# Two transformer layers on one core: the second MLP product in Strassen's plain form with a bank for each product, and a readiness rule for TensorE's order

## The chip, the core and the metric

The kernel runs on one core of a Trainium2 chip. A core has five engines that work side by side, each through its own instruction stream in program order: TensorE (PE, matrix products into PSUM), VectorE (DVE), ScalarE (ACT), GpSimd (POOL) and SyncE (SP, which here only issues transfers). They wait for each other by semaphores. Sixteen DMA engines move data between the HBM and the on-chip memory SBUF; here the transfers are issued from SP's and from ACT's stream. PSUM has eight banks of 2 KB for each of the 128 partitions. The metric is the time of one launch on the device in microseconds (us), lower is better.

## What is computed

The input is one sequence of 2048 rows of 640 float32 values. Two different blocks are applied alternately, each twice and with the same weights:

```python
x = x + _A_ref(_layernorm(x), A_wqkv, A_wo)
x = x + _B_ref(_layernorm(x), B_w1, B_b1, B_w2, B_b2)
x = x + _A_ref(_layernorm(x), A_wqkv, A_wo)
x = x + _B_ref(_layernorm(x), B_w1, B_b1, B_w2, B_b2)
```

Block A is attention with 32 heads of 20 values in which a row sees itself and the 255 rows before it. Block B is an MLP: `h = x @ w1 + b1` (640 to 1536), `h = max(h, 0) ** 2`, `h @ w2 + b2` (1536 to 640).

## The kernel before

**Number format.** Most products are made of three half-precision products: each operand is split into a high and a low float16 part, and high x high, high x low and low x high are summed in PSUM. The helper `mm3` (matmuls on L323) issues such a triple for each chunk of 128.

**Units.** The rows are cut into units of 256; with two layers there are 16 units (`NU`). The stages of a unit `u` are:

- `ln_load`, `ln_cross`: load the rows, layer norm, split into two float16 parts (`yl`) and turn them by transposing DMAs on SP into `yT` (L412, L434, L438, L441). There is one `yT` buffer.
- `stage_qk`, `stage_v`: the q, k and v projections from `yT`. q and k go to the HBM and come back in the layout for attention; `stage_v` works in four quarters of 15 matmuls.
- attention, in eight quads of four heads: `max_quad` (scores on L610, row maxima by DVE on L622), `exp_quad` (scores again on L673, exponential by ACT on L686, masks by POOL on L701 and L705) and `pv_quad` (product with v on L735, copy on L747). The maxima go to the rows of q through small transfers (`qt<-mT`, L648).
- `load_o`, `stage_o`: normalise the attention output, multiply with `wo`, add to the rows (L845), second layer norm; `y_cross` turns it into `y2`.
- `stage_f`: both MLP products, described next.

**The MLP in a unit.** The first product runs in six blocks `p`, each with feature chunks p and p + 6. ACT adds the bias and clips (L914), POOL squares (L918). The second product is a 2 x 2 block product in Strassen's way, with seven products for eight. Both sides need sums of blocks: those of `w2` are made once at the start and kept in the HBM (`w2d`); those of the activations are made in every block by POOL (L926, L930, L934), and ACT and DVE split the seven results into float16 parts (L937, L941) in the tile `hh`. Then come the seven products on L977, cut into 21 pieces of six matmuls; each piece needs 320 KB of `w2d`, fetched from ACT's stream (L311) into a ring of `SLOTS` = 7 places. The fetch for piece n + 7 is queued when piece n has been used. It is Winograd's form of the scheme: the products share sums. One bank, "x", stays open through four of the products, whose partial results build up in it; "y" is opened for the other three. DVE adds each result to the rows (L993). The bias `b2` is loaded anew in each unit and added by POOL in four halves (L865).

**Banks.** Six of PSUM's eight banks serve the scores of attention. The other two are handed out by `mm_tile` to all else: projections, MLP products, `pv`, small transposes.

**What sets the order.** The order of the instructions of every engine is fixed when the program is built. The builder keeps a clock `now` for TensorE and one for each other engine, with a booked cost for each operation. `post` queues a job for an engine; `pump` places the jobs whose start has come; `need` moves `now` forward until a job is done, that is, it accepts a wait of TensorE. `together` mixes attention with a stream of "dense" work (the generators of the stages above): after every attention step it runs dense work until that has had its share of the cost (`done < cost * share * part / total`). While "y" is open it runs dense work regardless. In loop `u`, the dense stream is q, k, v of unit u + 1, then `stage_o` and `stage_f` of unit u - 1.

## Time and profile before

| | us |
|---|---|
| runs shown | 1962.94 and 1966.79, median 1964.87 |
| the profiled execution | 1978.56 |
| its span, first to last instruction | 1976.8 |
| a steady unit (1315.3 to 1432.9) | 117.6 |
| its first MLP product (1369.7 to 1405.5) | 35.8 |
| its second MLP product (1405.5 to 1435.6) | 30.1 |

The profile comes from one profiled execution. PE is TensorE's matmuls and PEld its weight loads, which overlap them. A row of a table of groups reads: line, engine, operation, output<-inputs by the program's names, shape, xcount | busy us, mean ns of one | idle time of the engine just before them and what ended it. A row of the table of waits reads: who waited <- for whom: us in total, times, longest. A row of the timeline reads: start, length, engine, line, operation, xcount, and in brackets the idle time before it with what ended it. The granted clock (PEclk) is TensorE's clock as a share of full speed.

### The profile page before, as it was taken

The page shows a single profiled execution, that of the slowest core. Times are in us where ns is not written, and L with a number is a line of the kernel's source. Part 1 is how long each engine was busy: PE and PEld are TensorE (multiplying, and loading weights), DVE is VectorE, ACT ScalarE, POOL GpSimd, SP SyncE. Part 2 cuts the span into 40 slices and gives each one's busy share as a digit, 9 for nine tenths or more (in the row PEclk, how much of TensorE's full clock was granted, in tenths as well). Part 3 has the DMA queues.
Part 4 walks back from the last instruction along what each step waited for, and adds up shares of the span by engine and source line. Part 5 has one row for each costly group of instructions (what it writes and reads, how often), then busy time and mean ns, then how long its engine had stood idle before and what let it go on. Part 6 is the DMA issues. An engine that isn't in the chain of part 4 may idle for free. (4 is left out here: it accounts for less than half of the span.)

```text
span 1976.8 us, 44962 instructions
## 1 busy us (share of the span) xinstructions
PE 1700.5 (86%) x17398; PEld 1203.1 (61%) x17398; DVE 1106.3 (56%) x3230; ACT 757.8 (38%) x1509; POOL 832.0 (42%) x1594
## 2 busy tenths in 40 slices
PE   8976878898988989888897989889898898968878
PEld 7654556565656657566574756656666565645555
DVE  8776654565646456564455656456564555735342
ACT  4644334343443434434332433434344343434312
POOL 1236425345262533625243262524526244344524
PEclk9998989899989989899898989989999899988898
DMA  9765553745538275363747437274553836424253
GB/s 257 195 193 174 146 123 75 214 95 145 151 90 202 65 200 122 99 172 75 210 98 205 111 98 179 66 209 109 136 144 93 200 80 171 108 53 138 83 176 107
DMA packets 287982, 275.12 MB, mean 139 GB/s; under 512 B 87576, under 2 KB 228504, under 8 KB 287768
## 3 DMA queue, kind: packets, MB, share of 16 engines
q1 hardware_dynamic: 227640, 145.74, 31.6%
q10 hardware_dynamic: 60128, 126.51, 21.6%
q8 instruction: 137, 2.24, 0.5%
q14 instruction: 77, 0.63, 0.1%
HBM read 194.78 MB, written 59.83 MB: 129 GB/s over the span
## 5 line engine op out<-in xcount | busy, mean ns | idle before, releaser
L622 DVE CUSTOM_DVE_ANT_0 bb<-bb,maskb 128x384 f32<-128x384 f32 (+2 forms) x1024 | 512.1, 566 | 135.1 <-PE bb L610 120.3
L686 ACT ACTIVATE pt<-bb 128x512 f32<-128x512 f32 x736 | 377.5, 599 | 352.0 <-PE bb L673 247.2
L701 POOL TENSOR_SCALAR_AFFINE_SELECT pt<-pt 128x256 f32<-128x256 f32 x448 | 190.8, 432 | 620.8 <-ACT pt L686 613.0
L323 PE MATMUL acc<-y,w_s 128*128 128x256 f16 x2880 | 358.5, 288 | 12.7 <-ACT r L914 10.8
L977 PE MATMUL acc<-ring,hh 128*128 128x320 f16 x2016 | 304.6, 308 | 45.5 <-ACT hh L937 21.1
L323 PEld LDWEIGHTS <-w_s 128*128 128x128 f16 x2880 | 293.1, 103 | 81.5 <-issue 33.9
L323 PE MATMUL acc<-yT,wq_s 128*128 128x256 f16 x2250 | 290.9, 290 | 50.7 <-DMA yT<-yl 46.8
L323 PEld LDWEIGHTS <-wq_s 128*128 128x128 f16 x2400 | 244.0, 103 | 113.6 <-DMA yT<-yl 36.0
L735 PE MATMUL pv<-pt,vt 128*32 128x128 f32 (+1 forms) x3840 | 229.3, 348 | 74.3 <-POOL pt L705 41.2
L705 POOL TENSOR_SCALAR_AFFINE_SELECT pt<-pt 128x256 f32<-128x256 f32 x512 | 240.7, 492 | 107.2 <-ACT pt L686 103.2
L977 PEld LDWEIGHTS <-hh 128*128 128x128 f16 x2016 | 194.7, 100 | 149.6 <-issue 28.9
L941 DVE TENSOR_TENSOR hh<-r,hh 128x896 f16<-128x896 f32 x96 | 114.9, 1197 | 304.1 <-ACT hh L937 304.1
L735 PEld LDWEIGHTS pv<-pt,vt 128*32 128x32 f32 x3840 | 113.7, 114 | 149.8 <-POOL pt L705 67.3
L918 POOL TENSOR_TENSOR r<-r 128x256 f32<-128x256 f32 x192 | 132.6, 710 | 101.5 <-ACT r L914 99.8
L747 ACT COPY ot<-pv 128x256 f32<-128x256 f32 x128 | 47.6, 372 | 318.1 <-PE pv L735 280.2
L937 ACT CAST hh<-r 128x896 f16<-128x896 f32 x96 | 90.1, 938 | 179.5 <-POOL r L934 170.3
L360 POOL TENSOR_TENSOR bmv<-bmv,neghalf 128x1 f32<-128x1 f32 x64 | 42.7, 668 | 260.4 <-DVE bmv L354 260.3
L323 PE MATMUL acc<-wo_s,od 128*128 128x320 f16 x960 | 142.2, 301 | 7.6 <-DVE od L821 7.3
L673 PE MATMUL bb<-qt,kt 62*128 62x128 f16 (+1 forms) x1920 | 115.9, 246 | 36.5 <-DVE mx L622 16.8
L622 DVE DVE_READ_ACCUMULATOR2_ANT mx<- 128x1 f32 x1024 | 145.3, 142 | 0.0
L610 PE MATMUL bb<-kt,qt 60*128 60x128 f16 (+1 forms) x2176 | 113.6, 245 | 27.0 <-ACT pt L686 15.1
L323 PE MATMUL acc<-wq_s,yT 128*128 128x320 f16 x900 | 133.7, 301 | 3.0 <-DVE y L373 2.3
(97 smaller groups left out, 1469.8 us busy)
## 6 DMA issues: line engine op xcount, KB each, us to landing
ring<-w2d ACTq DMA_DIRECT2D x336, 320.0 KB
qt<-qk SPq DMA_DIRECT2D x30, 480.0 KB
kt<-qk SPq DMA_DIRECT2D x30, 480.0 KB
qk<-qd SPq DMA_DIRECT2D x17, 640.0 KB
o<-ot SPq DMA_DIRECT2D x256, 42.0 KB
od<-o SPq DMA_DIRECT2D x14, 640.0 KB
qk<-yl SPq DMA_DIRECT2D x13, 640.0 KB
w2d<-ring ACTq DMA_DIRECT2D x6, 1120.0 KB
```

The lines of the kernel that those rows point to most:

```text
L323: nc.tensor.matmul(acc, lhs(a, c), rhs(b, c), start=(k == 0), stop=(k == 3 * nk - 1))
L610: nc.tensor.matmul(to, qt[r, p, i * P:(i + 1) * P], kt[r, p, a:b], start=True, stop=True)
L622: nc.vector.tensor_tensor_reduce(out=v, in0=v, in1=mask, scale=1.0, scalar=-3.0e38, op0=ALU.add, op1=ALU.max, accum_out=accum),
L673: nc.tensor.matmul(bb[e][:, k, o:o + w], kt[r, 2 * qd + j, ko:ko + P], qt[r, 2 * qd + j, q0 * P:q0 * P + w], start=True, stop=True)
L686: nc.scalar.activation(box["pt"][:, :o], bb[e][:, k, :o], AF.Exp, scale=SCALE / (QS * QS))
L701: nc.gpsimd.affine_select(out=m, in_=m, pattern=[[0, 2], [-1, P]], compare_op=ALU.is_gt, fill=0.0, base=0, channel_multiplier=1)
L705: nc.gpsimd.affine_select(out=m, in_=m, pattern=[[0, 2], [1, P]], compare_op=ALU.is_ge, fill=0.0, base=0, channel_multiplier=-1)
L735: nc.tensor.matmul(pv[32 * jj:32 * (jj + 1), q0 * P:(q0 + qn) * P], vf[:, c:c + 32], pj[:, j, :], start=(k == 0), stop=(k == len(steps) - ...
L918: nc.gpsimd.tensor_tensor(blocks(), blocks(), blocks(), op=ALU.mult)
L937: nc.scalar.copy(hs[p // 3][:, 0, p % 3], box["r"][:, 0:7])
L941: nc.vector.tensor_sub(h[:, 1, p % 3], box["r"][:, 0:7], h[:, 0, p % 3])
L977: nc.tensor.matmul(acc[:, :HD], hs[p // 3][:, a, p % 3, PLACE[j], :], ring[:, n % SLOTS, c, b, :], start=bank not in started, stop=(p == F ...
```

## The change

It has five parts.

**Plain form.** The seven products are those of Strassen's first scheme. Each has its own bank, opened at its first piece and handed back when DVE has added it. A product is added to one to two places by `outs`; where two places have the same sign, one DVE instruction writes both. Nine adds cover twelve halves, where eight covered eight. Two squares and three sums on POOL become one square on ACT, one on DVE and three sums on POOL (two of 128x256, one of 128x128).

**Order.** Generators now yield a `Want` (jobs that must be done, and whether a bank must be free) ahead of what they need. `Stream.go` runs the dense stream until its next want isn't fulfilled in the program's clock. `together` goes on with attention when the quota is reached and the step's own wants are fulfilled, or when the dense stream can't go on and they are; otherwise time passes until either can.

**Where work lies.** The next unit's rows are loaded and normalised after block p = 0 of the first product instead of after the last. In loops u = 2 to 13, v's third quarter moves behind block 5 and the fourth ahead of the third product; the transposes into `yT` wait for that (`free`).

**Memory.** `SLOTS` is 6 for 7. `b2` is loaded once and stays; it is added in two instructions of 640 columns, queued behind the second layer norm. The two row tiles x1 become one, `xb`. The tile `r` has nine blocks for eight.

**Start and end.** w1's low halves are made by POOL with one more ACT pass in place of DVE; w2's sums follow the new scheme, its loads have other staging places and a higher priority; the first half of `hh` no longer waits for w2. The dense work held back for the last two units (`CARRY`, `KEEP`) goes from 25 and 27 thousand ns to 15 and 20.

```diff
-SLOTS = 7
+SLOTS = 6
...
+    def when(w):
+
+        if any(j.end is None for j in w.jobs):
+            return None
+        t = max([0.0] + [j.end for j in w.jobs])
+        if w.bank and len(banks2) > 1:
+            free = [max(j.end for j in b) + LAT for b in banks2 if b and all(j.end is not None for j in b)]
+            if not free:
+                return None
+            t = max(t, min(free))
+        return t
...
+    class Stream:
...
+        def go(self):
+            while not self.over:
+                if self.want is not None:
+                    t = when(self.want)
+                    if t is None or t > now[0]:
+                        return None
+                    self.want = None
+                c = next(self.gen, "over")
+                if c == "over":
+                    self.over = True
+                elif isinstance(c, Want):
+                    self.want = c
+                else:
+                    step(c)
+                    return c
+            return None
...
-    PIECES = [("x", 0, 0), ("x", 0, 1), ("y", 1, 0), ("y", 1, 1), ("x", 0, 2), ("y", 1, 2)] + [
-        (b, j, g) for b, j in (("x", 2), ("y", 3), ("x", 4), ("y", 6), ("x", 5)) for g in range(3)]
-    PLACE = [0, 1, 4, 6, 5, 2, 3]
+    PRODS = [(2, 3, [(1, 3, 1, 1)]), (1, 0, [(0, 1, 1, 1), (1, 2, 1, -1)]), (0, 6, [(1, 4, 2, 1)]), (3, 2, [(1, 2, 1, 1)]),
+             (6, 4, [(0, 3, 2, 1)]), (5, 1, [(2, 3, 1, -1), (3, 4, 1, 1)]), (4, 5, [(2, 3, 1, 1)])]
+    DONE = {3: [1], 4: [0], 5: [3], 6: [2]}
+    PIECES = [(0, 0), (0, 1), (1, 0), (1, 1), (0, 2), (1, 2)] + [(k, g) for k in range(2, 7) for g in range(3)]
...
-            out.append(dma(lambda turn=turn: turn(0), P * D * 2, j, cost=1250.0, land=CROSS))
+            out.append(dma(lambda turn=turn: turn(0), P * D * 2, j, after, cost=1250.0, land=CROSS))
...
-                    def square(blocks=blocks):
-                        nc.gpsimd.tensor_tensor(blocks(), blocks(), blocks(), op=ALU.mult)
+                    def square(blocks=blocks, k=k):
+                        if k:
+                            nc.vector.tensor_tensor(blocks(), blocks(), blocks(), op=ALU.mult)
+                        else:
+                            nc.scalar.activation(blocks(), blocks(), AF.Square)
...
+            if p == 0 and ahead is not None:
+                ln_load(ahead)
+            yield from between.get(p, ())
         if ahead is not None:
-            ln_cross(ahead, *b2j)
...
+            free = Job("S", 0.0, None, [], 0.0, 0)
+            ln_cross(ahead, free)
...
+            if k == 2 and g == 0 and FP in between:
+                yield from between[FP]
+                free.end = now[0]
+            yield Want(slots[n], hj[2 * g], bank=g == 0)
+            if g == 0:
+                accs[k] = mm_tile([P, 2 * T], "acc")
...
+        def work(part, w):
+
+            nonlocal done
+            while True:
+                t = when(w) if w else None
+                ready = t is not None and t <= now[0]
+                if done >= cost * share * part / total and (ready or not w):
+                    return
+                c = s.go()
+                if c is not None:
+                    done += c
+                elif ready or (s.over and not w):
+                    return
+                else:
+                    wait_any(*([w] if w else []), *([s.want] if s.want else []))
...
-            while opened["y"]:
-                c = next(dense)
-                step(c)
-                done += c
...
-    QKC, VC, OC, FCST, LNC, CARRY, KEEP, MID = 16.4e3, 8.2e3, 8.2e3, 36.8e3, 1.2e3, 25e3, 27e3, 8e3
+    QKC, VC, OC, FCST, LNC, CARRY, KEEP, MID = 16.4e3, 8.2e3, 8.2e3, 36.8e3, 1.2e3, 15e3, 20e3, 8e3
...
-            parts += [stage_qk(u + 1, (0,)), stage_v(u + 1, range(2)), stage_o(u - 1), lambda: (y_cross(u - 1), iter(()))[1], stage_qk(u + 1, (1,)), stage_v(u + 1, range(2, 4))]
+            parts += [stage_qk(u + 1, (0,)), stage_v(u + 1, range(2)), stage_o(u - 1), lambda: (y_cross(u - 1), iter(()))[1], stage_qk(u + 1, (1,))]
+            if u < NU - 2:
+                between = {FP - 1: stage_v(u + 1, (2,)), FP: stage_v(u + 1, (3,))}
+            else:
+                parts.append(stage_v(u + 1, range(2, 4)))
             cost += QKC + VC
```

311 lines of the change are left out of this document (173 added, 138 removed).

## The prediction

> **What bounds the kernel now.** I read the page's shares first.
>
> ```profile
> span 1976.8 us, 44962 instructions
> PE 1700.5 (86%) x17398; PEld 1203.1 (61%) x17398; DVE 1106.3 (56%) x3230; ACT 757.8 (38%) x1509; POOL 832.0 (42%) x1594
> ```
>
> TensorE is the bound, with two kinds of loss: it is idle for 1976.8 - 1700.5 = 276 us, and some of its busy time runs at a lower clock. No other engine is near full on average, so I asked which stage holds the loss. The next view is the table of windows for one steady unit (256 rows of one layer). Its columns are length, busy time of each engine with instruction counts, granted clock, DMA share and GB/s.
>
> ```profile
> core 0: us, PE busy (x) PEld busy (x) DVE busy (x) ACT busy (x) POOL busy (x), PEclk, DMA share, GB/s
> 1315.30:1432.90 117.60, 103.56 (x1109) 73.67 (x1108) 66.98 (x195) 46.42 (x92) 52.15 (x102) 0.96 0.55 137
> 1369.70:1405.50 35.80, 30.91 (x331) 22.77 (x328) 15.26 (x44) 15.27 (x30) 26.41 (x45) 0.95 0.28 60
> 1405.50:1435.60 30.10, 23.62 (x246) 15.52 (x244) 19.64 (x56) 10.51 (x20) 11.15 (x23) 1.00 0.85 215
> 1434.90:1438.30 3.40, 1.18 (x17) 0.76 (x18) 0.00 (x0) 0.00 (x0) 0.00 (x0) 1.00 1.06 226
> 1438.40:1441.70 3.30, 3.30 (x18) 2.32 (x17) 0.00 (x0) 3.04 (x6) 2.21 (x6) 0.50 1.03 371
> 1380.30:1383.70 3.40, 0.98 (x14) 0.29 (x8) 2.60 (x11) 0.71 (x1) 3.24 (x8) 1.00 0.00 0
> 1383.80:1387.10 3.30, 3.30 (x19) 1.80 (x19) 2.54 (x5) 0.50 (x2) 3.30 (x4) 0.50 0.02 5
> ```
>
> The first row is the unit. The second is the first MLP product: POOL is busy 26.4 of 35.8 us there, more than its average says. The third is the second MLP product: the DMA engines are 85% busy. The last four come in pairs: where TensorE worked only 1.2 or 1.0 us of 3.4, the next 3.3 us run at half clock. So a hole costs its own length and then about half of a stretch of 3.4 us. The view of the cores gives the mean over the run:
>
> ```profile
> core 0: 1976.8 us, clock 0.932
> ```
>
> So half-clock time is 2 x (1 - 0.932) x 1976.8 = 269 us, in which 134 us of full-speed work is lost. Which waits make the holes is in the table of waits (total us, times, longest), TensorE's own:
>
> ```profile
> PE acc L323 <- DMA yT<-yl: 46.8, 17, 10.5
> PE pv L735 <- POOL pt L705: 41.2, 40, 2.4
> PE pv L735 <- POOL pt L701: 25.3, 27, 1.9
> PE acc L977 <- ACT hh L937: 21.1, 14, 2.1
> PE bb L673 <- DVE mx L622: 16.8, 50, 1.8
> PE bb L610 <- ACT pt L686: 15.1, 20, 3.0
> PE acc L977 <- DVE hh L941: 12.3, 15, 1.0
> PE bb L610 <- DMA kt<-qk: 11.9, 2, 9.5
> PE pv L735 <- DVE x L993: 6.5, 13, 0.8
> PE acc L977 <- DMA ring<-w2d: 3.7, 5, 1.5
> ```
>
> **The change part by part.** The number of matmuls is untouched: seven products of 18 per unit before and after, so no term comes from arithmetic on TensorE.
>
> *A. Transposed layer norm, 33 us back.* The first row of waits is the q/k projection of the next unit waiting for its transposed input.
>
> ```profile
> 1402.77 0.82 SPq L412 DMA_DIRECT2D xt<-xs  x2
> 1415.77 6.72 SPq L441 DMA_TRANSPOSE yT<-yl  x2
> 1423.70 6.19 SPq L648 DMA_DIRECT2D qt<-mT  x4
> 1429.99 2.80 SPq L441 DMA_TRANSPOSE yT<-yl  x2
> 1437.56 0.28 PE L323 MATMUL acc<-yT,wq_s 128*128 128x256 f16 x1 [1.11 <-DMA yT<-yl]
> 1423.13 5.05 PE L977 MATMUL acc<-ring,hh 128*128 128x320 f16 x36
> ```
>
> The rows load at 1402.77, near the end of the first MLP product (1369.7 to 1405.5); the last transposes are issued from 1429.99 and TensorE starts on them at 1437.56. After the change the load is issued after the first of six blocks, some 25 us earlier, so the norm is done in time. But the four transposes now wait on SP until the last V quarter has read the old yT, just before the third product; behind them queue SP's row-maximum and output writes. From there: four issues of 2.80 / 2 = 1.4 are 5.6 us, and landing takes 1437.56 - 1432.79 = 4.8, together 10.4 us. TensorE still has 15 pieces of six matmuls, 15 x 5.05 / 6 = 12.6 us, plus attention. It fits by 2 us and more. Bounds: 0 to 46.8; I take seven tenths, since the first and last units keep another order.
>
> *B. GpSimd in the first MLP product, 40 us back.*
>
> ```profile
> L705 POOL TENSOR_SCALAR_AFFINE_SELECT pt<-pt 128x256 f32<-128x256 f32 x512 | 240.7, 492 | 107.2 <-ACT pt L686 103.2 <-PE acc L323 3.3
> L918 POOL TENSOR_TENSOR r<-r 128x256 f32<-128x256 f32 x192 | 132.6, 710 | 101.5 <-ACT r L914 99.8
> L930 POOL TENSOR_TENSOR r<-r 128x256 f32<-128x256 f32 x96 | 70.8, 738 | 6.6
> L865 POOL TENSOR_TENSOR x<-x,xt 128x320 f32<-128x320 f32 x60 | 60.5, 1033 | 1.0 <-DMA xt<-in_B_b_dram 1.0
> L926 POOL TENSOR_TENSOR r<-r 128x128 f32<-128x128 f32 x96 | 45.4, 473 | 7.4
> L934 POOL TENSOR_TENSOR r<-r 128x128 f32<-128x128 f32 x96 | 44.2, 460 | 6.4
> L914 ACT ACTIVATE r<-acc,b1s 128x256 f32<-128x256 f32 x192 | 80.7, 468 | 79.3 <-PE acc L323 73.6 <-DVE ring L292 2.6 <-DVE hh L941 2.3
> L941 DVE TENSOR_TENSOR hh<-r,hh 128x896 f16<-128x896 f32 x96 | 114.9, 1197 | 304.1 <-ACT hh L937 304.1
> ```
>
> One block now costs POOL 2 x 0.710 + 0.473 + 0.738 + 0.460 = 3.09 us (two squares, three sums). After, the squares are gone and the sums are two wide and one narrow: 2 x 0.72 + 0.47 = 1.91. The bias adds (4 x 1.03 = 4.1 us a unit, in the middle of the masks) become two double ones that are queued earlier, after the norm; same work, other place. So POOL's 26.4 us in this stage fall by 6 x 1.18 + 4.1 = 11.2, and attention's masks (L701, L705), for which pv waits 66.5 us, come through sooner. I take 40, between 0 and 66.5: three fifths, as some of these waits lie outside this stage. What it costs elsewhere: a square of 128x256 on ACT by the nearest row 0.47 us, 96 x 0.47 = 45 us; on DVE, by the add of 128x320 below, up to 0.49, 96 x 0.49 = 47 us. The squares of a block run side by side, so its chain is not longer: 2 x 0.47 + 3.09 + ACT's copy + 1.20 before, 2 x 0.47 + 0.47 + 1.91 + the same after. I book them at nothing; TensorE's blocks cover them. Uncovered, they would be up to 45 us.
>
> A rule stands against this. A select of the same shape takes 0.41 us where it runs freely, and 0.492 in the mean of L705.
>
> ```profile
> 1378.00 0.41 POOL L705 TENSOR_SCALAR_AFFINE_SELECT pt<-pt 128x256 f32<-128x256 f32 x1
> ```
>
> The Trainium skill, GPSIMD Engine Reference, section Specifications, says that GpSimd's SBUF interfaces are shared with VectorE and contend with its two-input instructions, and VectorE's new square reads two SBUF inputs. If each of the 96 held GpSimd up for its whole length and all of that reached TensorE, by that rule the time would be some 47 us higher; the spread of the selects agrees that something stretches them, and does not show what.
>
> *C. End of the first product, 25 us back.* The L977 waits for hh (21.1 + 12.3 = 33.4) come from the last block's chain. Two V quarters (15 matmuls of 0.14, so 2.1 us each) are now put after the last block and before the third product in 12 of 16 units; 2.1 just covers the mean of 33.4 / 16 = 2.1 us a unit, and attention may stand there too. 12/16 of 33.4 is 25; bounds 0 and 33.
>
> *D. Clock, 45 us back.* A, B and C take away 98 of 276 us of idle time. I give the clock a third of its 134 us; bounds 0 and two thirds, 90.
>
> *E. Own banks and more adds.*
>
> ```profile
> L993 DVE SCALAR_TENSOR_TENSOR x<-acc,x 128x320 f32<-128x320 f32 x120 | 57.4, 489 | 62.9 <-PE acc L977 60.7
> L622 DVE CUSTOM_DVE_ANT_0 bb<-bb,maskb 128x384 f32<-128x384 f32 (+2 forms) x1024 | 512.1, 566 | 135.1 <-PE bb L610 120.3 <-ACT pt L686 7.2 <-ACT vt L567 5.7
> L622 DVE DVE_READ_ACCUMULATOR2_ANT mx<- 128x1 f32 x1024 | 145.3, 142 | 0.0
> ```
>
> Eight adds of one half a unit become nine that cover twelve halves: 4 x 0.49 x 16 = 31 us more DVE. With the squares DVE goes to about 1184 us, 60%. An add ends while the next product (18 matmuls, 2.5 us) runs in the other bank. Zero on the path; bounds -10 (the waits of pv for x go) and +56 (below).
>
> *F. Six ring slots for seven, 32 us lost.*
>
> ```profile
> 1303.11 5.51 DMA ring<-w2d
> ```
>
> This row of the chain of waits is a fetch landing after 5.51 us. A fetch is issued when its slot's piece is done and must land before six other pieces are; now five: 5 x 0.84 = 4.2 us instead of 5.05, plus attention between. One piece is 128 x 1280 values of 2 bytes, 0.328 MB; at the 215 GB/s of the window that is 1.52 us, against 0.84 of matmuls. Bounds: 0, and (1.52 - 0.84) x 15 = 10 us a unit. I take 2 us x 16, near the lower end, by the 3.7 us that ring waits cost now.
>
> *G. Ends, 13 us back.* Less dense work is held back for the last unit, so that attention near the end has company (L610's 15.1 + 11.9): 10 of 27. At the start w1's low halves leave DVE for POOL: 3. Bounds -7 (KEEP is 7 thousand ns smaller, work that could have stood beside the last unit's loads) and 27.
>
> Sum: 33 + 40 + 25 + 45 + 13 - 32 = 124 us. The profiled execution took 1978.56 us (its span and 1.8 around it), 13.7 above the median of the runs shown; 1978.6 - 124 = 1854.6 there, and 1841 against the median of 1964.87.
>
> **The rivals.**
>
> *All holes close.* Ready work always fills them: D reaches 90, the waits for mx (16.8) and the rest of A (13.8) go too, 1841 - 45 - 17 - 14 = 1765. Against it: the DMA share near 1 at the unit's end.
>
> *The ring becomes the bound.* Five pieces of lead are less than the landing time, and TensorE waits 6 of F's upper 10 us a unit, 4 more than booked: 1841 + 64 = 1905. For it: 5.51 against 4.2, and 85% DMA share. Against: the V quarter gives the ring time to fill, and attention lies between the pieces.
>
> *Banks turn too slowly.* Each of 7 x 16 product starts waits 0.5 us (6.5 / 13, what pv waits for x now) for the bank's add, 56 us, and the small holes keep the clock down, 45: 1841 + 101 = 1942. The row for the second product shows clock 1.00 with three of seven products in a bank that turns, which speaks against it. The Trainium skill, TensorE: Matmul & The Clock Gate, section A second HAM failure mode: psum-queue depth-cycling, describes just that: cycling banks gives small idle times and the clock falls.
>
> *The order stays what it was.* The quota of dense work per attention step remains, and readiness only adds to it. If it decides everywhere, A, D and half of B are not had: 1841 + 33 + 45 + 20 = 1939. Against it: in the second product the old code ran dense work on while a bank was open, and that is gone.
>
> *The program's clock is early: slower.* The order is now taken from estimates, and these are short: it books 0.515 us for a maximum over 384 where the rows show 0.566 + 0.142. Eight a quad are 8 x 0.19 = 1.5 us. If TensorE is sent to a quad as soon as the program calls it ready, and stands there 1.5 us in each of 128 quads, that is 192 us: 1841 + 192 = 2033. From 1 us a quad on it eats the gain of 124 and decides. Against it: the same estimates place the waits now, and mx costs TensorE only 16.8 us.
>
> **How the numbers follow.** Chances: forecast 0.52, all close 0.10, ring 0.11, banks 0.07, order as before 0.07, clock early 0.13. The forecast's own range is 1795 (D at 90) to 1890 (the rule on GpSimd's port). The range 1775 to 1950 leaves out the clock-early case and part of the best one, 0.2 in all. Two per cent, about what a measurement can tell from no change, is 1926 to 2004: faster gets the forecast, the best case, nearly all of the ring's and some of the next two, 0.76; same 0.12; slower 0.12.
>
> **What would show it.** A: no hole ahead of the first yT matmuls, transposes issued before the third product. B: POOL near 15 us in the first product's stage, pv waits under 30. C: L977 no longer waiting for hh. D: mean clock at 0.95. F: ring waits of TensorE near 30 us. A clock that stays at 0.93, ring waits above 100 us, or mx and mask waits above 100 us would make the prediction wrong.

## The result and the profile after

The changed kernel takes 1735.49 us (median of two runs, 1731.19 and 1739.80) against 1964.87 before. The ratio is 0.8833, with a 95% interval of 0.8731 to 0.8934. The forecast was 1841, its range 1775 to 1950: the direction is right and the gain, 229 us, is nearly twice the 124 that the sum had. The time lies below the range, and the nearest rival is "all holes close" with 1765.

The profiled execution of the changed kernel took 1739.8 us. The head of its page and its view of the cores, in the columns used before:

```profile
span 1737.6 us, 45200 instructions
PE 1605.9 (92%) x17398; PEld 1171.6 (67%) x17398; DVE 1171.2 (67%) x3330; ACT 792.6 (46%) x1617; POOL 762.8 (44%) x1382
```

```profile
core 0: 1737.6 us, clock 0.970
```

The number of matmuls is the same, 17398. The span fell by 1976.8 - 1737.6 = 239.2 us, some 10 more than the medians, as the profiled execution before was a long one. These two rows split it. TensorE's idle time went from 276.3 to 1737.6 - 1605.9 = 131.7, which is 144.6 less. Its busy time went from 1700.5 to 1605.9, 94.6 less for the same matmuls. Most of that is clock: half-clock time is now 2 x (1 - 0.970) x 1737.6 = 104 us, 165 less than the 269 before, and half of that, 82, is work won back; the other 12.6 is left open.

The next view is the windows of long stretches: first the kernel before, eleven units (from the end of unit 0's second product to that of unit 11's), then the changed kernel, thirteen units measured the same way, with what lies ahead of them and behind.

```profile
245.40:1551.40 1306.00, 1148.31 (x11934) 812.81 (x11933) 729.10 (x2159) 499.69 (x996) 560.68 (x1090) 0.94 0.54 135
```

```profile
254.20:1567.00 1312.80, 1262.93 (x14168) 927.91 (x14168) 916.67 (x2629) 615.45 (x1262) 594.31 (x1118) 1.00 0.59 155
0.00:254.20 254.20, 208.68 (x2023) 151.73 (x2024) 176.14 (x513) 121.91 (x241) 109.72 (x164) 0.89 0.67 189
1567.00:1737.60 170.60, 134.25 (x1213) 91.92 (x1213) 78.34 (x189) 55.21 (x114) 58.79 (x100) 0.87 0.33 108
```

Before, a steady unit took 1306.0 / 11 = 118.7 us, with (1306.0 - 1148.3) / 11 = 14.3 of idle and a clock of 0.94. Now it takes 1312.8 / 13 = 101.0, with 3.8 of idle and a clock of 1.00. That is 17.7 us a unit, of which 10.5 are idle time and 7.2 are clock. Unit 0 got no faster (its second product ends at 254.2, before at 245.4). What loss is left has moved to the two ends: of 104 us at half clock, 2 x 0.11 x 254.2 = 56 are in the first stretch and 2 x 0.13 x 170.6 = 44 in the last.

One steady unit of the changed kernel, with its first and its second MLP product as the second and third row:

```profile
1158.00:1258.30 100.30, 97.97 (x1111) 72.06 (x1109) 71.83 (x204) 47.95 (x98) 46.98 (x88) 1.00 0.59 158
1198.50:1227.50 29.00, 28.72 (x328) 22.93 (x328) 19.36 (x54) 19.14 (x41) 19.51 (x35) 1.00 0.42 99
1227.50:1258.10 30.60, 29.23 (x327) 19.25 (x326) 21.31 (x60) 11.63 (x23) 11.69 (x26) 1.00 0.81 233
```

In the first product TensorE was idle 4.9 of 35.8 us and is now idle 0.3 of 29.0. POOL's work there fell from 26.4 to 19.5 us. In the second product it was idle 6.5 of 30.1 and is now idle 1.4 of 30.6, which holds more attention work (327 matmuls for 246).

The table of waits of the changed kernel, TensorE's own, the seven largest, and two further down that the prediction spoke of:

```profile
PE bb L730 <- DVE mx L679: 30.4, 47, 6.6
PE bb L667 <- ACT pt L743: 18.4, 32, 3.5
PE acc L1045 <- DMA ring<-w2d: 11.7, 16, 1.6
PE acc L374 <- ACT od L875: 10.9, 2, 7.8
PE acc L1045 <- ACT ot L804: 8.9, 13, 0.7
PE acc L1045 <- DVE hh L1004: 6.7, 16, 0.9
PE acc L1045 <- ACT hh L1000: 5.4, 4, 2.5
...
PE pv L792 <- POOL pt L762: 1.3, 2, 0.7
...
PE acc L1045 <- DVE x L1059: 0.9, 1, 0.9
```

The waits for `yT` (46.8) are gone from the table, those of pv for masks fell from 66.5 to 1.3, and those of the MLP's products for `hh` from 33.4 to 12.1. The ring rose from 3.7 to 11.7. Waits for the row maxima rose from 16.8 to 30.4. The row `<- ACT ot` (8.9 us in 13 waits) was 0.5 before: in the steady unit above it stands between a pv group and the next product, whose bank the program can give out only when ACT has copied pv out of it (`ot`):

```profile
1232.57 2.47 PE L1045 MATMUL acc<-ring,hh 128*128 128x320 f16 x17 [0.74 <-ACT ot L804]
```

### The profile page after: what moved, and what is told of

The parts are those of the page before. It is cut to its first block, busy times and chain, and to the rows that moved or that the text cites. A ratio compares the mean times of both kernels' runs of the same rounds, so it can differ in the third digit from the quotient of the medians.

```text
span 1737.6 us, 45200 instructions
## 1 busy us (share of the span) xinstructions
PE 1605.9 (92%) x17398; PEld 1171.6 (67%) x17398; DVE 1171.2 (67%) x3330; ACT 792.6 (46%) x1617; POOL 762.8 (44%) x1382
## 5 line engine op out<-in xcount | busy, mean ns | idle before, releaser
L374 PE MATMUL acc<-y,w_s 128*128 128x256 f16 x2880 | 333.5, 275 | 4.5 <-DVE y L425 2.2
L1045 PE MATMUL acc<-ring,hh 128*128 128x320 f16 x2016 | 302.7, 302 | 36.7 <-DMA ring<-w2d 11.7
L374 PEld LDWEIGHTS <-w_s 128*128 128x128 f16 x2880 | 281.3, 99 | 56.8 <-issue 21.1
L374 PE MATMUL acc<-yT,wq_s 128*128 128x256 f16 x2250 | 262.4, 274 | 1.6 <-DVE yl L556 0.8
L374 PEld LDWEIGHTS <-wq_s 128*128 128x128 f16 x2400 | 231.9, 98 | 45.8 <-issue 15.6
L792 PE MATMUL pv<-pt,vt 128*32 128x128 f32 (+1 forms) x3840 | 192.7, 335 | 1.4 <-POOL pt L762 1.3
L1004 DVE TENSOR_TENSOR hh<-r,hh 128x896 f16<-128x896 f32 x96 | 110.3, 1149 | 64.1 <-ACT hh L1000 62.6
L730 PE MATMUL bb<-qt,kt 62*128 62x128 f16 (+1 forms) x1920 | 115.8, 248 | 33.3 <-DVE mx L679 30.4
L989 POOL TENSOR_TENSOR r<-r 128x256 f32<-128x256 f32 x96 | 77.0, 802 | 151.7 <-DVE r L979 95.6
L792 PEld LDWEIGHTS pv<-pt,vt 128*32 128x32 f32 x3840 | 106.2, 111 | 50.1 <-issue 13.0
L374 PEld LDWEIGHTS <-od 128*128 128x128 f16 x960 | 91.6, 99 | 62.6 <-issue 12.3
L730 PEld LDWEIGHTS <-kt 62*128 62x128 f16 x1920 | 73.9, 95 | 74.8 <-issue 56.5
```

The costliest lines, as they stand in the source:

```text
L374: nc.tensor.matmul(acc, lhs(a, c), rhs(b, c), start=(k == 0), stop=(k == 3 * nk - 1))
L730: nc.tensor.matmul(bb[e][:, k, o:o + w], kt[r, 2 * qd + j, ko:ko + P], qt[r, 2 * qd + j, q0 * P:q0 * P + w], start=True, stop=True)
L792: nc.tensor.matmul(pv[32 * jj:32 * (jj + 1), q0 * P:(q0 + qn) * P], vf[:, c:c + 32], pj[:, j, :], start=(k == 0), stop=(k == len(steps) - ...
L989: nc.gpsimd.tensor_tensor(r[:, 2:4], r[:, 0:2], r[:, 7:8].to_broadcast([P, 2, P]), op=ALU.add)
L1004: nc.vector.tensor_sub(h[:, 1, p % 3], box["r"][:, 1:8], h[:, 0, p % 3])
L1045: nc.tensor.matmul(acc[:, :HD], hs[p // 3][:, a, p % 3, place, :], ring[:, n % SLOTS, c, b, :], start=p == 0 and z == 0, stop=p == FP - 1 ...
```

## The experiments

Each kernel was timed in turn with the kernel before on the same chip, and its ratio is against that; the interval behind a ratio is its 95% interval. To set two kernels beside each other I take the difference of their ratios times 1964.87, and call that the difference in us. Line numbers shift by a few between kernels.

**The changed kernel again**, unaltered, as the base for all that follows.

> The changed kernel unaltered, to narrow its ratio (0.8833, from 0.873 to 0.893). If the small differences are real, it comes out at 0.882 to 0.885, above v3's 0.8755 and its interval; if they lie in the spread of chips and launches, anywhere down to 0.876.

1738.43 us, ratio 0.8826 (0.8793 to 0.8858). Its ring row has 14.1 us where the first profile had 11.7, which shows how far such a row moves by itself.

### The early norm and the V quarters, taken back

`e3_no_v_fill` puts all V quarters back to their old place, so that the transposes wait for nothing; `e4_late_norm` also loads the next unit's rows after the last block again.

```diff
-            if u < NU - 2:
+            if False:
                 between = {FP - 1: stage_v(u + 1, (2,)), FP: stage_v(u + 1, (3,))}
...
-            if p == 0 and ahead is not None:
-                ln_load(ahead)
...
+            ln_load(ahead)
             free = Job("S", 0.0, None, [], 0.0, 0)
```

> The changed kernel with all four V quarters in their old place ahead of the second MLP, so that nothing stands between the blocks and the products, and the transposes wait for nothing. WORK: TensorE waits for hh again at the start of the products, 2 to 3 us a unit and perhaps half of a stretch at half clock: 30 to 60 us slower. ORDER: attention is put there, under 15 us slower.

> As e3_no_v_fill, and the next unit's rows are loaded only after the sixth block, as before the change. WORK: the q/k projection waits for its transposes again, 3 us idle and 3.4 us at half clock a unit on top of e3, 13 x 4.7 = about 60 us slower than e3. ORDER: no other dense work exists at that place, so part of it shows under this theory too, but attention fills it: under 25 us slower than e3.

`e3_no_v_fill` takes 1769.43 us, 0.9001 (0.8941 to 0.9060): 34 us slower than the changed kernel. The waits of TensorE in it:

```profile
PE acc L1045 <- ACT hh L1000: 37.0, 17, 3.0
...
PE acc L1045 <- DVE hh L1004: 14.0, 18, 1.0
```

Behind the first product's end TensorE now stands for 37.0 / 17 + 14.0 / 18 = 3.0 us in the mean unit, in two pieces, and the clock of the run falls from 0.970 to 0.958. `e4_late_norm` takes 1890.54 us, 0.9611 (0.9558 to 0.9665): 120 us more than `e3_no_v_fill`, twice what was expected. Its waits, its timeline of TensorE where one unit ends, and the windows there:

```profile
PE acc L374 <- DMA yT<-yl: 77.6, 23, 6.7
```

```profile
1148.95 0.37 PE L374 MATMUL acc<-yT,wq_s 128*128 128x256 f16 x1 [4.78 <-DMA yT<-yl]
...
1153.09 7.17 PE L374 MATMUL acc<-yT,wq_s 128*128 128x256 f16 x44 [3.76 <-DMA yT<-yl]
```

```profile
1144.20:1149.00 4.80, 0.05 (x1) 0.08 (x1) 0.00 (x0) 0.00 (x0) 0.00 (x0) 0.83 1.44 196
1149.00:1152.50 3.50, 0.33 (x1) 0.03 (x1) 0.00 (x0) 3.04 (x6) 2.35 (x7) 0.50 0.69 79
1153.10:1160.00 6.90, 6.90 (x44) 5.32 (x44) 0.69 (x1) 0.60 (x1) 0.07 (x1) 0.67 0.61 206
```

Two holes of 4.78 and 3.76 us, and the 44 matmuls behind them at a clock of 0.67, cost 8.5 + 0.33 x 6.9 = 10.8 us in this unit. The same late norm cost 46.8 us of waits in all in the kernel before. My reading is that there the unit's other holes gave the norm time; once they are closed, TensorE reaches the end of the unit sooner and the norm is no sooner done.

In the changed kernel both are in place, and the timelines of SP and of TensorE show it:

```profile
1206.55 0.82 SPq L465 DMA_DIRECT2D xt<-xs  x2
1238.77 5.79 SPq L495 DMA_TRANSPOSE yT<-yl  x4
```

```profile
1255.06 3.19 PE L1045 MATMUL acc<-ring,hh 128*128 128x320 f16 x21
1258.09 1.80 PE L374 MATMUL acc<-yT,wq_s 128*128 128x256 f16 x15
```

The rows are loaded 8 us into the first product, the transposes are issued from 1238.77, some 19 us ahead of their first reader, and no idle time stands ahead of the `yT` matmuls.

### GpSimd's work and the early norm, alone in the kernel before

`b1_before_light_gpsimd` only moves the squares, `b2_before_early_norm` only the norm, `b3_before_both` does both.

```diff
-    def ln_cross(u, *deps):
...
-        ln_load(u, *deps)
+    def ln_cross(u):
...
-                        nc.gpsimd.tensor_tensor(blocks(), blocks(), blocks(), op=ALU.mult)
+                        if k:
+                            nc.vector.tensor_tensor(blocks(), blocks(), blocks(), op=ALU.mult)
+                        else:
+                            nc.scalar.activation(blocks(), blocks(), AF.Square)
...
+            if p == 0 and ahead is not None:
+                ln_load(ahead, *b2j)
...
-            ln_cross(ahead, *b2j)
+            ln_cross(ahead)
```

> The kernel before, with the two squares of a block on ACT and DVE; Winograd form, banks and order as before. By the terms of the prediction: pv's waits for the masks (66.5 us) fall by 40 and the clock gives some 15 back, 0.97 of before (1910). Theory CHAIN (the waits of a unit stand one behind the other; what ends earlier in the MLP is lost again at the unit's end, where the transposed norm is the last to come): under 20 us faster, with the wait for yT grown.

> The kernel before, with the next unit's rows loaded after the first of the six blocks; its transposes wait for nothing but yT's readers. By the waits of before: 33 to 47 us of idle time and 1.7 to 3.4 us of clock a unit, 50 to 80 us faster (about 1900). CHAIN: the same, as this is the last of the chain. If the transposes themselves (DMA near its limit at that place) are late: under 20 us.

> The kernel before with the edits of b1 and b2. ADD: the sum of the two gains. CHAIN: more than the sum, because the early norm lets the time won in the MLP through: 110 to 150 us faster (about 1835).

| | us | ratio | gain |
|---|---|---|---|
| squares off GpSimd | 1886.38 | 0.9598 (0.9556 to 0.9640) | 79 |
| early norm | 1913.19 | 0.9722 (0.9687 to 0.9757) | 55 |
| both | 1847.65 | 0.9400 (0.9370 to 0.9431) | 118 |

The waits of TensorE that answer, in `b1_before_light_gpsimd` and then in `b2_before_early_norm`:

```profile
PE acc L323 <- DMA yT<-yl: 42.4, 19, 10.3
PE bb L673 <- DVE mx L622: 29.9, 74, 1.5
...
PE pv L735 <- POOL pt L705: 8.6, 14, 0.9
```

```profile
PE pv L733 <- POOL pt L703: 41.1, 40, 2.4
...
PE pv L733 <- POOL pt L699: 25.3, 27, 1.9
```

Each edit takes its own wait away, wholly or nearly so, and leaves the other's nearly as it was (42.4 for 46.8; 66.4 for 66.5), and the two gains nearly add: 134 against 118 for both; more than the sum, as the theory CHAIN had it, did not come. So in the kernel before the two are worth half of the change's gain. Two squares cost POOL 2 x 0.71 = 1.42 us a block; without them pv's waits for masks fall from 66.5 to 9.9 (8.6 and 1.3 on the other mask line) and the clock of the profiled execution rises from 0.932 to 0.966. The waits for the maxima grow from 16.8 to 29.9 and take part of it back.

### Does GpSimd's load still matter in the changed kernel?

`e1_order_blind` takes the program's clock out of the readiness rule (only free banks count); `e2_squares_gpsimd` puts both squares back on POOL; `e5_blind_and_gpsimd` does both; `e7_gpsimd_late_bias` is the second with the two bias adds queued at the start of the MLP, as before.

```diff
-        if any(j.end is None for j in w.jobs):
-            return None
-        t = max([0.0] + [j.end for j in w.jobs])
+        t = 0.0
...
-            t = max(t, min(free))
...
-                        if k:
-                            nc.vector.tensor_tensor(blocks(), blocks(), blocks(), op=ALU.mult)
-                        else:
-                            nc.scalar.activation(blocks(), blocks(), AF.Square)
+                        nc.gpsimd.tensor_tensor(blocks(), blocks(), blocks(), op=ALU.mult)
...
-            add_b2(u, i, x1, ys[u, i][1])
...
+            add_b2(u, i, xbs[u][:, i * D:(i + 1) * D], None)
```

> The changed kernel, but the readiness rule looks only at whether a PSUM bank can be had; jobs that are not done no longer hold a step back (TensorE waits for them where it stands). Theory ORDER (the readiness rule closes the holes): most of the gain goes, at least 100 us slower than the changed kernel's 1735, clock back to about 0.94. Theory WORK (the holes closed because what TensorE waited for now comes earlier: less on GpSimd, earlier norm, V quarters): within 20 us of 1735, clock above 0.96.

> The changed kernel with both squares of a block on GpSimd again, all else as changed. WORK: the waits of pv for the masks return, 4 to 5 us of idle a unit and half of one 3.4 us stretch at half clock, 6.5 x 14 = about 90 us slower (1825). ORDER: the rule puts other work ahead of pv while GpSimd is late, at most 25 us slower.

> The changed kernel with both edits of e1_order_blind and e2_squares_gpsimd. Theory COVER (readiness and the lighter GpSimd each remove the waits of pv for the masks, so each alone could be taken back cheaply): the two together bring these waits back, at least 40 us in the table of waits and 60 to 100 us slower than e1 alone (about 1840). Theory ADD (the costs simply add: 10 for the squares, 29 for the order): about 1775.

> As e2_squares_gpsimd, and the two bias adds of b2 (1.8 us each) are queued at the start of the MLP again, so that GpSimd has all that it had there before the change. Theory LUMP (the bias adds in the middle of the masks made the waits of pv): 50 to 80 us slower than e2 (about 1810), with pv's waits for the masks back. Theory ORDER (readiness puts dense work before pv while GpSimd is late): within 20 us of e2.

| | us | ratio |
|---|---|---|
| order blind | 1764.32 | 0.8956 (0.8887 to 0.9025) |
| squares on GpSimd | 1745.40 | 0.8864 (0.8816 to 0.8912) |
| both | 1777.77 | 0.9068 (0.9020 to 0.9116) |
| squares on GpSimd, bias adds late | 1737.09 | 0.8833 (0.8810 to 0.8856) |

The blind order costs 26 us, just outside the 20 that the theory WORK allowed and far from the 100 of ORDER. By its profile the loss is idle time and not clock: TensorE is idle for 149.2 us (131.7 in the changed kernel) at a clock of 0.983 (0.970). In its table of waits the maxima and the exponentials grow, as they should if TensorE is sent to steps that aren't ready:

```profile
PE bb L727 <- DVE mx L676: 41.3, 75, 5.1
PE bb L664 <- ACT pt L740: 37.9, 35, 12.5
```

The squares on POOL, worth 79 us in the kernel before, cost nothing here that can be told from the base, nor do the late bias adds, and pv waits 0.3 and 0.9 us for masks. With the blind order too, 48 us are lost against 26 + 7 for the parts, which the intervals don't tell apart, and pv waits 2.2 us for masks where the theory COVER had 40. So neither the lighter load nor readiness alone is what keeps the masks on time, and something else in the change does.

### The priority of the MLP's jobs

That something is in the calls of `post`, and it is a sixth part of the change, which the five parts named ahead of the prediction leave out. The kernel before queues the MLP's squares, sums and splits with `prio=0`, ahead of attention's jobs; the changed kernel leaves the default. `e8_priority_back` is `e7_gpsimd_late_bias` with the old priority, `e9_priority_back_blind` adds the blind order, and `b4_before_priority` drops the priority in the kernel before.

```diff
-                    js.append(post("G", 571, square, j))
+                    js.append(post("G", 571, square, j, prio=0))
...
-                j = post("G", 690, s1, *js)
-                j = post("G", 690, s2, j)
-                j = post("G", 420, s3, j)
-                j = post("A", 825, high, j)
-                hj.append(post("D", 1050, low, j))
+                j = post("G", 690, s1, *js, prio=0)
+                j = post("G", 690, s2, j, prio=0)
+                j = post("G", 420, s3, j, prio=0)
+                j = post("A", 825, high, j, prio=0)
+                hj.append(post("D", 1050, low, j, prio=0))
```

> The kernel before, in which only the queue priority of the MLP's squares, sums and splits is the default, as that of attention's masks; all of GpSimd's work stays. Theory PRIORITY (masks stood behind the MLP's jobs in GpSimd's queue): most of b1's gain, 50 to 85 us faster than before (about 1900), the waits of pv for the masks (66.5) below 20. Theory AMOUNT (GpSimd has too much to do): under 20 us.

> As e7_gpsimd_late_bias (all of GpSimd's old work), and the MLP's jobs first in the queues again. PRIORITY alone decides: pv's waits for the masks come back, 50 us or more slower than e7 (1737). Readiness covers it: within 25 us of e7, pv's waits under 15.

> As e8_priority_back with the rule of e1_order_blind, so that GpSimd has its old work in its old order and nothing moves in TensorE's order. PRIORITY: pv's waits above 30 us and 40 to 80 us slower than e5_blind_and_gpsimd (1778). If neither priority nor amount matters with the new form of the MLP: within 20 us of e5.

`e8_priority_back` takes 1820.68 us, 0.9243 (0.9201 to 0.9286), 81 us more than without the priority; `e9_priority_back_blind` takes 1904.58, 0.9693 (0.9658 to 0.9729), 123 more than `e5_blind_and_gpsimd`. The priority holds for the splits on ACT and DVE too: the ring's waits are 24.5 us in `e8_priority_back` for 12.3 in `e7_gpsimd_late_bias`, and how much of the 81 is POOL's queue alone is not separated. The mask waits are back, in `e8_priority_back` and then in `e9_priority_back_blind`:

```profile
PE pv L792 <- POOL pt L758: 26.7, 27, 2.5
PE pv L792 <- POOL pt L762: 10.3, 15, 1.9
```

```profile
PE pv L789 <- POOL pt L755: 64.5, 59, 2.6
...
PE pv L789 <- POOL pt L759: 14.1, 21, 1.9
```

Three things can thus keep the masks on time: less work on POOL, the masks ahead of the MLP in POOL's queue, and an order on TensorE that runs something else until they are done. With one of the first two the waits are nearly gone (9.9 in `b1_before_light_gpsimd`, 0.3 in `b4_before_priority` below, 2.2 in `e5_blind_and_gpsimd`); readiness alone halves them (78.6 to 37.0). That is why taking back one of the three shows so little.

In the kernel before, the priority alone gains nothing that can be told: `b4_before_priority` takes 1960.70 us, 0.9979 (0.9945 to 1.0014). Its table of waits shows where 66 us went:

```profile
PE acc L323 <- DMA yT<-yl: 106.4, 21, 10.5
PE acc L977 <- ACT hh L937: 33.9, 15, 3.0
```

Of pv's waits for masks 0.3 us is left, as the theory PRIORITY had it, but its gain of 50 to 85 us did not come: the wait for `yT` grew by 60, that for `hh` from ACT by 13. To tell whether that is the late norm, `b5_before_priority_norm` adds the early norm of `b2_before_early_norm` to it.

> The kernel before with the edits of b4_before_priority and b2_before_early_norm; GpSimd's work unchanged. CHAIN: the early norm lets through what the priority gives, about 115 us faster than before (1850, like b3), against 5 and 54 for the two alone. ADD: 54 + 5, about 1906. AMOUNT still counts: between, with pv's waits back.

1905.69 us, 0.9701 (0.9656 to 0.9745): 55 us better, no more than the early norm alone. The wait for `yT` is still there, and the timelines of POOL and SP show why:

```profile
PE acc L323 <- DMA yT<-yl: 51.8, 19, 5.5
```

```profile
1334.43 1.69 POOL L863 TENSOR_TENSOR x<-x,xt 128x320 f32<-128x320 f32 x2
```

```profile
1335.29 1.19 SPq L412 DMA_DIRECT2D xt<-xs  x2
```

In the kernel before, `ln_load` is given the bias adds (`b2j`) to wait for, which need POOL. Without priority the last two adds come only at 1334.43, and both of the norm's loads (x2) stand behind: the first at 1335.29, when the first of the two adds is done and 27 us after the unit's first product began. In `b2_before_early_norm` the first load comes 2.4 us into the product. In the changed kernel `ln_load(ahead)` waits for no bias add. Dropping the priority is worth 81 us there, in `e8_priority_back` against `e7_gpsimd_late_bias`, and nothing in the kernel before; a norm that hangs on POOL's queue is the difference that the rows show, and whether it is the only one was not tried.

### Five places in the ring

```diff
+USED = 5
...
-            fetch(n + SLOTS, used_)
+            fetch(n + USED, used_)
```

> The changed kernel with five ring places in use for six. The prediction booked 32 us for the step from seven to six; if the lead of the ring decides, one place less costs at least as much again, 32 us or more (1767), and the ring row in the table of waits rises from 11.7 to above 40. If the V quarters and attention between the pieces cover the fetches: under 15 us.

The ring's index goes modulo `USED` as well, and the tile keeps its six places. 1745.09 us, 0.8869 (0.8836 to 0.8903), which can't be told from the base. Waits on the ring:

```profile
PE acc L1046 <- DMA ring<-w2d: 18.1, 21, 2.4
```

One place less costs 18.1 - 11.7 = 6.4 us of waits, or 4.0 against the 14.1 of the changed kernel's second profile. So the step from seven to six is not likely to have cost 32.

### The ends

In the last two units the changed kernel uses up its dense work while attention waits, and has none left beside the last attention steps. The row of TensorE's timeline for the last `stage_o` shows a hole of 7.79 us ahead of it:

```profile
1668.76 10.80 PE L374 MATMUL acc<-wo_s,od 128*128 128x320 f16 x60 [7.79 <-ACT od L875]
```

`v1_keep_reserve` stops the dense stream in the last two units at its share while the attention step's end is known; `v3_blind_end` switches the program's clock off in the last two units alone, `v5_blind_end3` in the last three.

```diff
+    blind = [False]
...
-        if any(j.end is None for j in w.jobs):
+        if not blind[0] and any(j.end is None for j in w.jobs):
             return None
-        t = max([0.0] + [j.end for j in w.jobs])
+        t = 0.0 if blind[0] else max([0.0] + [j.end for j in w.jobs])
...
-            t = max(t, min(free))
+            t = t if blind[0] else max(t, min(free))
...
+        blind[0] = u >= NU - 2
```

The core of `v1_keep_reserve` is in `work`:

```diff
-                c = s.go()
+                full = share < 1.0 and done >= cost * share and t is not None
+                c = None if full else s.go()
```

> The changed kernel, but in the last two units the dense stream stops at the share that is set aside (CARRY, KEEP) as long as attention's next step is known, instead of running on whenever attention isn't ready. In the changed kernel all dense work is used up before the last attention ends, and TensorE then stands 7.8 us before the last output projection. If that is why its ends take 273 us from the 13th unit on against 254 with e1, this gains 10 to 20 us (about 1720); if the reserve only moves idle time to the place where it is saved, within 5.

> The changed kernel, with the rule of e1_order_blind in the last two units only (readiness as changed in the others). By the lengths of e1's units: its steady units cost 2.9 us more each, its last three together 19 less, so 15 to 20 us faster than the changed kernel (about 1717). If the ends are quick only because e1's earlier units left more work over: no gain.

> As v3_blind_end, with readiness off in the last three units for the last two. If the gain lies in unit 13 as well (where e1 does more attention): 5 to 10 us faster than v3's 1719. If readiness is worth its 2.9 us in every unit that has V quarters: 3 us slower than v3.

| | us | ratio |
|---|---|---|
| reserve kept | 1737.59 | 0.8844 (0.8831 to 0.8857) |
| blind in the last two units | 1719.19 | 0.8755 (0.8734 to 0.8776) |
| blind in the last three units | 1726.04 | 0.8786 (0.8754 to 0.8818) |

Keeping a reserve brings nothing: TensorE stands 2.0 us ahead of the last `stage_o` for 7.8, but 4.7 for 3.1 ahead of the one before it and 4.4 for 1.0 in the products between them. Blind in the last two units is the fastest kernel here, 14 us better than the changed kernel, with the intervals apart; blind in the last three can be told from neither of the two, so its two theories stay undecided. The clock of the profiled execution is 0.983 by its view of the cores. So readiness costs 14 us at the end and earns some 26 + 14 = 40 in the rest, if the two add (the blind order everywhere lost 26). That it loses at the end because there is too little dense work to choose from is a reading, not shown.

## Why the prediction fell short

The direction and the outline of the mechanism were right: holes in TensorE's stream close, and clock comes with them. The sum was too small, and in step B what keeps the masks on time was in part another thing. Its signs come out so: no hole ahead of the first `yT` matmuls; mask waits 1.3 (under 30); POOL 19.5 us in the first product's stage (15 forecast; the sums there got longer, as the last section shows); waits for `hh` 12.1, though none were to be left; clock 0.970 (0.95); ring waits 11.7 (30). The sizes failed, and by profile they sum so: of idle time 79 us were booked (33 + 40 + 25 + 13 - 32) and 144.6 came; of clock 45 were booked, 82 came back by the clock, and 94.6 came off the busy time. Of the 66 us of idle time too few, the tables of waits put 59 on four terms: A booked 33 of the 46.8 for `yT` and all went (14 short), B booked 40 of the 66.5 for masks and 65.2 went (25 short), F booked a loss of 32 and the ring's waits grew by 8 (24 short), and C booked 25 where 21.3 went (4 too many). So the steps that failed are the shares taken in A and B, the loss in F and the third taken in D. By step:

- **A, 33 us.** The step took the waits for `yT` in the old table as the upper bound. Alone in the kernel before the early norm gains 55 (`b2_before_early_norm`): 44.3 of the 46.8 us of waits go, and some clock comes back; with the unit's other holes closed it is worth 120 (`e4_late_norm`). Once what lies ahead of a wait at the end of a chain gets shorter, the wait can grow (77.6 us in `e4_late_norm`), so the old table's row was no bound on what the edit is worth.
- **B, 40 us.** The reason, POOL's load, gives 79 alone (`b1_before_light_gpsimd`). But the step missed the priority in `post`, and in the changed kernel that keeps the masks on time without the lighter load (`e7_gpsimd_late_bias`, then `e8_priority_back`). I had worked out POOL's time in the stage, and not the order in its queue. Booking the squares' new places at nothing is not contradicted: in the changed kernel no difference can be told by where they run.
- **C, 25 us.** 34 by `e3_no_v_fill`, which includes its clock. Right in place and nearly in size; the waits for `hh` themselves fell by 21.3.
- **D, 45 us.** I gave the clock a third of 134 because a good third of the idle time would go. 82 came back. How much idle time goes does not set it: `e1_order_blind` is idle for longer than the changed kernel (149.2 us) at a higher clock (0.983). In the steady unit shown no wait of TensorE is longer than 0.7 us, and the clock there is 1.00, as the windows show. What is left of half-clock time is at the ends.
- **E, zero.** For the adds it stands as far as the waits tell: product starts waited 0.9 us for a bank's add in the whole run. But the step left out that pv takes the same two banks: the waits for ACT's copy of pv are 8.9 us. The rival in which banks turn too slowly, and with it the fall of the clock of which the Trainium skill, TensorE: Matmul & The Clock Gate, section A second HAM failure mode: psum-queue depth-cycling, tells, did not come: banks change at each of the seven products and the third window of the steady unit has a clock of 1.00. The new form of the product was not run alone.
- **F, 32 us lost.** Too cautious: ring waits rose by 8, and a further place less costs 4 to 6 more. Dense work is now spread over more attention (327 matmuls for 246 in the stage), which would give each fetch more time than five pieces of matmuls; that this is the reason was not tried.
- **G, 13 us.** Unit 0 is 9 us later than before. From the end of unit 11's second product (1551.4 before, 1360.6 after) to the end of the span it is faster by (1976.8 - 1551.4) - (1737.6 - 1360.6) = 48, some 12 for each of the last four units, less than the 18 of a steady one, so no gain of the ends can be singled out; `v3_blind_end` shows 14 us still lying there.

The readiness rule had no term of its own; it stood only in two rivals. By `e1_order_blind` it is worth 26 net. The rival in which the program's clock is early and TensorE stands 1.5 us at each quad, 192 us in all, is refuted by the 30.4 us of waits for maxima, and of the 47 us of the rule on GpSimd's port nothing is seen in the time: with DVE's square back on POOL (`e2_squares_gpsimd`) nothing is won.

**One way to add it up.** The runs form a chain from the kernel before to the changed kernel, in which each step is the difference of two ratios:

| step | from and to | us |
|---|---|---|
| early norm | before, `b2_before_early_norm` | 55 |
| V quarters, plain form and banks, ring of six, `b2` loaded once, start and end, and all else | `b2_before_early_norm`, `e9_priority_back_blind` | 6 |
| priority (and the place of the bias adds) | `e9_priority_back_blind`, `e5_blind_and_gpsimd` | 123 |
| squares off GpSimd | `e5_blind_and_gpsimd`, `e1_order_blind` | 22 |
| readiness | `e1_order_blind`, `a0_changed_again` | 26 |

Together they are 231 us. The second step can't be told from nothing (0.9722 and 0.9693, the intervals overlap). The largest is the priority, for which the prediction has no term. In another order the shares come out otherwise: the priority alone in the kernel before gave nothing, and the early norm is worth 120 at the other end.

**What stays open.** The plain form with its own banks, the single bias load and the new `CARRY` and `KEEP` were not tried alone. In the second step they stand together with the V quarters, whose gain (34 in the changed kernel) may be hidden there by the waits for masks, so a gain or a loss of theirs is not shown.

## What to carry to other kernels

A table of waits prices a wait only as long as all else stands: when 66 us of one wait were closed, the next in the chain grew by 60, and a wait of 46.8 was worth 120 once the holes ahead of it were gone, so cost an edit in the schedule that the other edits make. For an engine with one queue look at the priority of what stands in it before its load: the same squares cost 79 us in the kernel before, where they went ahead of the masks, and nothing that can be told in the changed one, where they don't. Count clock by stretch (in the windows here it is 0.50 behind a long hole and 1.00 in a unit without one), and ask which stretches will have no long hole left.

## What the hardware showed

**The clock falls by hole, and comes back whole.** Thirteen steady units with 3.8 us of idle time each, in small pieces, ran at 1.00; eleven with 14.3 ran at 0.94. In `e3_no_v_fill` two stops of 3.0 us together in the mean unit were enough to bring the run from 0.970 to 0.958. In one of its units the stops are 3.03 us, up to 1161.64, and 0.97 us; a window that holds the first, and one behind both:

```profile
1158.60:1162.00 3.40, 0.37 (x4) 0.11 (x2) 1.04 (x2) 3.35 (x7) 3.40 (x8) 1.00 0.49 183
1165.50:1168.90 3.40, 3.40 (x46) 1.90 (x40) 2.79 (x11) 0.00 (x0) 0.00 (x0) 0.50 0.92 229
```

**POOL's sums got longer.** The groups of the changed kernel, POOL's three sums:

```profile
L989 POOL TENSOR_TENSOR r<-r 128x256 f32<-128x256 f32 x96 | 77.0, 802 | 151.7 <-DVE r L979 95.6 <-ACT r L974 38.6 <-ACT r L981 17.4
L993 POOL TENSOR_TENSOR r<-r 128x256 f32<-128x256 f32 x96 | 80.3, 837 | 0.0
L997 POOL TENSOR_TENSOR r<-r 128x128 f32<-128x128 f32 x96 | 60.4, 629 | 0.0
```

A sum of 128x256 took 0.738 us before and now 0.80 to 0.84, one of 128x128 0.460 to 0.473 and now 0.629. The Trainium skill, GPSIMD Engine Reference, section Specifications, says that GpSimd's SBUF interfaces are shared with VectorE and that VectorE's instructions with two SBUF inputs contend, and VectorE's new square is such a one. But the square is not what these runs show as the cause. The sums in `b1_before_light_gpsimd`, with the square on DVE and the old priority, and then in `b4_before_priority`, with both squares on POOL and the priority dropped:

```profile
L933 POOL TENSOR_TENSOR r<-r 128x256 f32<-128x256 f32 x96 | 70.8, 738 | 7.3
L937 POOL TENSOR_TENSOR r<-r 128x128 f32<-128x128 f32 x96 | 45.0, 469 | 6.6
```

```profile
L930 POOL TENSOR_TENSOR r<-r 128x256 f32<-128x256 f32 x96 | 79.1, 824 | 6.6
L926 POOL TENSOR_TENSOR r<-r 128x128 f32<-128x128 f32 x96 | 69.2, 721 | 5.4
```

With the square on DVE the sums are as short as before; with the priority alone dropped two of the three are longer (the third, L934, takes 0.458). With the squares back on POOL in the changed kernel (`e2_squares_gpsimd`) the first wide sum takes 1.053 us, the second 0.794 and the narrow one 0.462. So the length of POOL's sums moves with the order of the work and what then runs beside them, and which instruction holds up which stays open. TensorE waits for these sums only by way of `hh`, and that wait fell all the same (33.4 to 12.1).
